# Scores of two heads in the two 64-row halves of TensorE, the projection's sums spread over steps, and two small sums moved

## The chip, the cores and the metric

The kernel runs on one core of a Trainium2 chip. A core has a matrix engine (PE, with its weight loads PEld shown apart), VectorE (DVE), ScalarE (ACT), GpSimd (POOL) and queues that start DMA transfers (SP's here, and ACT's for the output). The metric is the device time of one execution in microseconds (us); the median of several runs counts.

## The reference, cut to what matters

```
# r, k, v: (4, 8, 768, 48) float32;  w, u: (8, 48)
for t in range(S):
    cur = einsum('bhd,bhe->bhde', u * k_t, v_t)
    y[:, :, t] = einsum('bhd,bhde->bhe', r_t, state + cur)
    state = w * state + einsum('bhd,bhe->bhde', k_t, v_t)
x = y as (3072, 384)
out = (silu(x @ w_gate) * (x @ w_val)) @ w_out     # d_ff = 1536
```

The weights are between 0.85 and 0.95, so the recurrence can be done in chunks of 128 time steps with scaled copies of k and r.

## The kernel before, in words

**Chunks.** There are 24 chunks `i`: 6 stretches of 128 time steps times 4 batches, and chunk `i` works on batch `i % 4`. For a chunk, POOL makes `khat = k * kscale` and `rhat = r * rscale` (function `scale`, L274 and L275; `kscale` and `rscale` hold powers of w and are made once at the start). `turn` (L300 to L308) transposes both on PE, two heads at a time: a pair is 2 x 48 = 96 columns, so the transposed `kT` and `rT` have 96 rows, 48 of each head. ACT copies them out of PSUM. For `kT` it does so twice (L303), once per head of the pair, scaling each time by a column of `own`, which is 1 on the rows of that head and 0 on the other's.

**Scores.** `scores(i, half)` multiplies four such zeroed `kT` by `rT` (L314, 128 columns out, 96 rows deep), and DVE copies what lies on the right side of the diagonal into `At` (`copy_predicated`, L318). `diagonal` has filled `At` before with the sums `du` on the diagonal (L291 on ACT, eight heads each). `own_product` makes `rk = r * k * u` on POOL (L202, L203) and sums it over a head's 48 numbers on DVE (L205) into `du`, both at the same place of the program.

**Outputs and state.** `outputs` (L344) multiplies `At` by v and `rT` by the state `Z` in four 32-column strips of PE, which a line of code addresses by 32 rows of the result each. `update` (L357 on PE, L367 or L369 on DVE, L370 on POOL) adds the chunk's keys and values to `Z`.

**The second block.** 12 groups `g` of two chunks go through `gate_value` (L390 on PE, L396 on ACT, L397 and L398 on DVE) and `project` (L453). The projection is done with seven products of half blocks instead of eight. This needs four sums of the weight's blocks, made once (`weight_sums`, L414 to L417 on POOL, 1152 numbers a row each), and four sums of h's blocks for each group (`h_sums`, L432 to L435 on POOL, for the last group on DVE).

**The weights** come as 64-bit floats and are rounded to 32 bits in 18 parts on the core: ACT (L162, L166), DVE (L179, L180) and POOL (L190), a part at a time. `round_weights` advances this by one part. It writes to a PSUM tile `w_mag` of which there is one.

**The order** is written out by hand: every engine executes its instructions in the order in which the program calls them. Step `s` calls, in this order: `diagonal(s-1)`, `own_product(s+1)`, `scale(s+1)`, `turn(s)`, `scores(s-1)` in two halves, `outputs(s-2)` and `update(s-2)`. Between these stand `gaps`, which hold pieces of the second block (`feed`, taken from the list `todo`) and, in steps 3 to 11, rounding of weights:

```
EARLY = {s: ("R", "F", "R", "F", "RF") for s in range(3, 12)}
```

R is `round_weights`, F one piece of `todo`. From step 12 on the five gaps hold 3, 2, 2, 3 and 2 pieces. A piece of `todo` waits until enough weights are rounded; those that need the sums of the weights wait for `NW + 1`, that is for `weight_sums` to stand in the program.

`ps_a` has four PSUM buffers that the tiles `tp` (twice), `s_ps` (twice), `y_ps` and `u_ps` of a step take in turn, so `y_ps` takes the buffer that the transposed `khat` of its step had, and the next `tp` those of the scores.

Of the kernel before, what the change touches and what calls it, by code (L numbers as in the profile page):

```python
# [15 lines left out]
P = 128  # L16
# [6 lines left out]
def fast(  # L23
# [44 lines left out]
    wcol = cst.tile([D2, HP], FP32, name="wcol")  # L68
# [3 lines left out]
    own = cst.tile([D2, 2], FP32, name="own")  # L72
    wL = cst.tile([D2, HP, 2, D], FP32, name="wL")
    sq = cst.tile([D2, 8, HP], FP32, name="sq")
    bad = cst.tile([D2, HP], FP32, name="bad")
    held = cst.tile([D2, HP], FP32, name="held")
    badc = cst.tile([D2, 1], FP32, name="badc")
    ones = cst.tile([D2, 1], FP32, name="ones")
# [7 lines left out]
    Z = [cst.tile([D2, HP, D2], FP32, name=f"Z{b}") for b in range(B)]  # L86
# [110 lines left out]
    dus = {}  # L197

    def own_product(i):
        kl, rl = k_ld[i % 2], r_ld[i % 2]  # L200
        rk = two.tile([P, H, D], FP32, name="rk", tag="rk")
        pool.tensor_mul(rk[:], rl[:], kl[:])  # L202
        pool.tensor_mul(rk[:], rk[:], ub[:])  # L203
        du = three.tile([P, H], FP32, name="du", tag="du")
        dve.tensor_reduce(du[:], rk[:], axis=AX.X, op=ALU.add)  # L205
        dus[i] = du
# [3 lines left out]
    for t in v_ld:  # L210
        dve.memset(t[:, :, D:64], 0.0)
    for e in range(2):
        sp.dma_start(out=wcol[D * e : D * e + D, :], in_=w.rearrange("(a e) d -> e d a", e=2)[e])
# [23 lines left out]
    for step, base in ((-D, 0), (D, D - 1)):  # L237
# [8 lines left out]
    pw = two.tile([D2, HP, P + 1], FP32, name="pw", tag="hT")  # L246
    dve.memset(pw[:, :, P : P + 1], 1.0)
    dve.tensor_copy(pw[:, :, P - 1 : P], held[:].unsqueeze(2))
    for l in range(7):
        n = 1 << l  # L250
        f = sq[:, l, :].unsqueeze(2).to_broadcast([D2, HP, n])
        dve.tensor_mul(pw[:, :, P - 2 * n : P - n], pw[:, :, P - n : P], f)
    for n in (1, 0):
        t_ps = ps_a.tile([P, HP, D2], FP32, name="t_ps", tag="a")
        for a in range(HP):
            pe.transpose(t_ps[:, a, :], pw[:, a, n : n + P], ident[0:D2, 0:D2])
        x = t_ps[:].rearrange("p a x -> p (a x)")
        if n:
            act.copy(kscale[:].rearrange("p h d -> p (h d)"), x)
        else:  # L260
            dve.reciprocal(rscale[:].rearrange("p h d -> p (h d)"), x)
    own_product(0)
    own_product(1)

# [8 lines left out]
    def scale(i):  # L273
        pool.tensor_mul(khat[i % 4][:], k_ld[i % 2][:], kscale[:])  # L274
        pool.tensor_mul(rhat[i % 2][:], r_ld[i % 2][:], rscale[:])  # L275
# [20 lines left out]
    def turn(i):  # L296
        for nm, t in (("kT", khat[i % 4]), ("rT", rhat[i % 2])):
            tp = ps_a.tile([P, HP, P], FP32, name="tp", tag="a")
            for a in range(HP):
                pe.transpose(tp[0:D2, a, :], pair(t, a), ident[:])  # L300
            if nm == "kT":
                for e in range(2):
                    act.activation(  # L303
                        kT[i % 2][:, :, e, :], tp[0:D2], AF.Identity, scale=own[:, e : e + 1]
                    )
            else:
                turned[i] = three.tile([D2, HP, P], FP32, name=nm, tag=nm)
                act.copy(turned[i][:], tp[0:D2])  # L308

    def scores(i, half):  # L310
        ps = ps_a.tile([P, HP, P], FP32, name="s_ps", tag="a")
        for n in range(4):
            a, e = divmod(4 * half + n, 2)
            pe.matmul(  # L314
                ps[:, n, :], kT[i % 2][:, a, e, :], turned[i][:, a, :],
                start=True, stop=True, skip_group_check=True,
            )
        dve.copy_predicated(  # L318
            At[i % 2][:, 4 * half : 4 * half + 4],
            mask[:].bitcast(INT32).unsqueeze(1).to_broadcast([P, HP, P]), ps[:],  # L320
        )
# [28 lines left out]
    def update(i):  # L350
# [4 lines left out]
        ps = ps_a.tile([D2, HP, D2], FP32, name="u_ps", tag="a")  # L355
# [15 lines left out]

    def count_outside():

        dve.tensor_tensor(bad[:], held[:], wcol[:], ALU.not_equal)
        dve.tensor_reduce(badc[:], bad[:], axis=AX.X, op=ALU.add)
        dve.memset(ones[:], 1.0)
        n_ps = ps_a.tile([P, HP, P], FP32, name="n_ps", tag="a")
        pe.matmul(n_ps[0:1, 0, 0:1], badc[:], ones[:], start=True, stop=True)
        act.copy(outside, n_ps[0:1, 0, 0:1])
# [33 lines left out]
    def weight_sums():  # L413
        pool.tensor_sub(wt[1][:], w22, w12)  # L414
        pool.tensor_sub(w12, w12, w11)
        pool.tensor_sub(wt[0][:], w22, w12)
        pool.tensor_sub(wt[2][:], w21, wt[0][:])  # L417
# [8 lines left out]
    def h_sums(g, by):  # L426
        a, b = (
            three.tile([P, 2, FH, P], FP32, name=n, tag="w_bits") for n in ("hs12", "hs34")
        )
        h11, h12, h21, h22 = h_quarters(g)  # L430
        s1, s2, s3, s4 = a[:, 0], a[:, 1], b[:, 0], b[:, 1]
        by.tensor_add(s1, h22, h21)  # L432
        by.tensor_sub(s2, s1, h11)
        by.tensor_sub(s3, h11, h21)
        by.tensor_sub(s4, h12, s2)  # L435
        part_of[g] = {"s": (s1, s2, s3, s4)}
# [556 lines left out]
```

## Time and profile before

| what | value |
|---|---|
| median of 3 runs (lowest, highest) | 706.93 us (706.92, 707.24) |
| the profiled execution: its time, its span | 708.06 us, 706.3 us |
| mean granted TensorE clock | 0.988 |
| DVE, ACT, POOL busy | 240.7 us (34%), 204.4 us (29%), 237.1 us (34%) |
| scores L314: matmul records | 384, 51.3 us |
| outputs L344: matmul records | 768 with `At`, 480 with `Z` |
| state L357: matmul records | 160, 16.6 us |

One matmul of 32-bit floats stands in the trace as two records, one for each of two passes, with two weight loads; a transpose stands as one. A record's duration has the depth of the array in it and overlaps the next one's. What a group of matmuls takes out of PE's time is the distance from its first start to the start of what follows, and it is that distance which is used below. "idle before ... <- X" says what ended a wait. The span is counted from the first to the last instruction.

### The profile page before, as it was taken

The numbers are of one execution on the slowest core, as the hardware profiler recorded it, in microseconds if no ns is written. First come the engines' busy times: TensorE is split into PE (matmuls) and PEld (weight loads), VectorE is DVE, ScalarE is ACT, GpSimd is POOL, SyncE is SP. The second block draws the span as 40 slices with busy tenths as digits, with TensorE's granted clock in tenths as the row PEclk, the third lists the DMA queues.
The fourth block names the chain that finished last, engine by engine and source line by source line (L and its number), as shares of the span: only waits on it lengthen the run. The fifth ranks groups of instructions, "written<-read, shape, count | busy, mean of one in ns | idle before, by whom it ended". The sixth has DMA issues, their size and how long they took to land.

```text
span 706.3 us, 11610 instructions
## 1 busy us (share of the span) xinstructions
PE 681.0 (96%) x4822; PEld 620.2 (88%) x4822; DVE 240.7 (34%) x519; ACT 204.4 (29%) x522; POOL 237.1 (34%) x191
## 2 busy tenths in 40 slices
PE   8888997999899999999999999999999999999996
PEld 8777886898798998999999999999898998998996
DVE  5777772313222222323222322323222322222222
ACT  3577762442132231313131331313131211111110
POOL 6877678358203320602512420602400400304000
PEclk9998998999999999999999999999999999999999
DMA  8798831113001010102011110001000000000000
GB/s 236 196 240 226 204 76 34 35 35 78 17 18 46 12 34 23 34 1 57 12 23 35 23 35 23 12 1 35 1 1 23 1 1 23 1 17 7 1 23 26
DMA packets 85774, 34.07 MB, mean 48 GB/s; under 512 B 76368, under 2 KB 79568, under 8 KB 85712
## 3 DMA queue, kind: packets, MB, share of 16 engines
q1 hardware_dynamic: 82256, 28.52, 17.3%
q10 hardware_dynamic: 3456, 4.72, 1.8%
q8 instruction: 40, 0.66, 0.4%
q14 instruction: 22, 0.18, 0.1%
HBM read 28.51 MB, written 4.72 MB: 47 GB/s over the span
## 4 chain that ended last, share of the span: by engine, by line
PE 81%; DVE 6%; POOL 5%; ACT 5%; issue 1%; DMA 1%; SPq 0%; DVEq 0%; POOLq 0%
PE gv L390 47%; PE o_a L453 13%; PE o_b L453 10%; PE y_ps L344 4%; PE s_ps L314 4%; PE tp L300 2%; ACT At L291 2%; ACT w_mag L162 1%; PE u_ps L357 1%; DVE At L318 1%; ACT kT L303 1%; DVE hT L398 1%; DVE sg L397 1%; DVE wg L180 1%; DMA r_ld<-in_r_dram 1%
## 5 line engine op out<-in xcount | busy, mean ns | idle before, releaser
L390 PE MATMUL gv<-xT,wg 128*128 128x256 f32 x864 | 216.0, 387 | 4.0 <-DVE hT L398 4.0
L390 PE MATMUL gv<-xT,wv 128*128 128x256 f32 x864 | 211.6, 381 | 0.0
L390 PEld LDWEIGHTS gv<-xT,wv 128*128 128x128 f32 x864 | 165.5, 192 | 22.9
L390 PEld LDWEIGHTS gv<-xT,wg 128*128 128x128 f32 x864 | 159.7, 193 | 25.8 <-issue 7.7
L397 DVE TENSOR_TENSOR sg<-sg,gv 128x256 f32<-128x256 f32 x144 | 60.5, 420 | 348.2 <-ACT sg L396 347.8
L396 ACT ACTIVATE sg<-gv 128x256 f32<-128x256 f32 x144 | 55.0, 382 | 345.9 <-PE gv L390 345.8
L432 POOL TENSOR_TENSOR hs<-hT 128x768 f32<-128x768 f32 x11 | 19.9, 1809 | 195.6 <-DVE hT L398 195.6
L370 POOL TENSOR_TENSOR Z<-Z,wL 96x384 f32<-96x384 f32 x16 | 15.9, 995 | 191.7 <-DVE Z L369 191.7
L398 DVE TENSOR_TENSOR hT<-sg,gv 128x256 f32<-128x256 f32 x144 | 60.6, 421 | 5.1
L291 ACT ACTIVATE At<-ident,du 128x128 f32<-128x128 f32 x176 | 53.6, 389 | 0.0
L314 PE MATMUL s_ps<-rT,kT 96*128 96x128 f32 x384 | 51.3, 278 | 0.4 <-DVE Z L367 0.4
L453 PE MATMUL o_a<-wt,hs 128*128 128x192 f32 x288 | 50.9, 327 | 0.4 <-ACT u L461 0.4
L314 PEld LDWEIGHTS s_ps<-rT,kT 96*128 96x128 f32 x384 | 49.5, 194 | 1.5 <-DVE Z L367 0.7
L453 PE MATMUL o_b<-wo,hs 128*128 128x192 f32 x288 | 50.7, 326 | 0.0
L453 PEld LDWEIGHTS o_a<-wt,hs 128*128 128x128 f32 x288 | 47.5, 190 | 1.5 <-ACT u L461 0.7
L453 PEld LDWEIGHTS o_b<-wo,hs 128*128 128x128 f32 x288 | 47.6, 190 | 0.8
L318 DVE COPY_PREDICATED At<-mask,s_ps 128x512 f32<-128x512 int32 x48 | 35.0, 733 | 24.4 <-PE s_ps L314 24.4
L344 PE MATMUL y_ps<-At,v_ld 128*32 128x128 f32 x768 | 36.1, 279 | 5.8 <-ACT kT L303 4.4
L344 PEld LDWEIGHTS y_ps<-At,v_ld 128*32 128x32 f32 x768 | 29.9, 111 | 6.6 <-ACT kT L303 4.6
L344 PE MATMUL y_ps<-rT,Z 96*32 96x128 f32 x480 | 30.2, 278 | 1.7 <-ACT kT L303 1.7
L303 ACT ACTIVATE kT<-tp,own 96x512 f32<-96x512 f32 x48 | 29.8, 672 | 0.0
L162 ACT ACTIVATE w_mag<-w_bits 128x384 f32<-128x384 f32 x36 | 19.0, 529 | 24.3 <-DVE wg L180 11.0
(82 smaller groups left out, 639.2 us busy)
## 6 DMA issues: line engine op xcount, KB each, us to landing
k_ld<-in_k_dram SPq DMA_DIRECT2D x24, 192.0 KB, 2.9
r_ld<-in_r_dram SPq DMA_DIRECT2D x24, 192.0 KB, 3.3
w_bits<-in_moe_w_gate_dram SPq DMA_DIRECT2D x6, 768.0 KB, 5.1
v_ld<-in_v_dram SPq DMA_DIRECT2D x48, 96.0 KB, 2.8
w_bits<-in_moe_w_val_dram SPq DMA_DIRECT2D x6, 768.0 KB, 4.7
w_bits<-in_moe_w_out_dram SPq DMA_DIRECT2D x6, 768.0 KB, 4.5
out_dram<-o_sb ACTq DMA_DIRECT2D x24, 192.0 KB, 1.9
ub<-in_u_dram SPq DMA_DIRECT2D x1, 192.0 KB, 3.7
```

Of the source, the lines that this page charges most:

```text
L162: act.activation(mags[n][-1].bitcast(FP32), hi.bitcast(FP32), AF.Abs, scale=float(2.0**-112))
L291: act.activation(At[i % 2][:, h, :], ident[:], AF.Identity, scale=du[:, h : h + 1])
L303: act.activation(kT[i % 2][:, :, e, :], tp[0:D2], AF.Identity, scale=own[:, e : e + 1])
L314: pe.matmul(ps[:, n, :], kT[i % 2][:, a, e, :], turned[i][:, a, :], start=True, stop=True, skip_group_check=True,)
L318: dve.copy_predicated(At[i % 2][:, 4 * half : 4 * half + 4], mask[:].bitcast(INT32).unsqueeze(1).to_broadcast([P, HP, P]), ps[:],)
L344: pe.matmul(ps[32 * q : 32 * q + 32, cc, :], *rows[q][n], start=(n == 0), stop=(n == len(rows[q]) - 1), skip_group_check=True,)
L390: pe.matmul(gv[:, o, :].rearrange("p (i t) -> p i t", i=2), wt[:, c, P * f : P * (f + 1)], xT[:, 2 * g % NX : 2 * g % NX + 2, c, :], start ...
L396: act.activation(sg[:], gv[:, 0, :], AF.Sigmoid)
L397: dve.tensor_mul(sg[:], sg[:], gv[:, 0, :])
L398: dve.tensor_mul(hT[g][:, f, :], sg[:], gv[:, 1, :])
L432: by.tensor_add(s1, h22, h21)
L453: pe.matmul(ps[:], lhs[:, f, :], rhs[:, f, :], start=(f == 0 and n in (0, 1, 4)), stop=(f == FH - 1), skip_group_check=True,)
```

## The change

Six things are changed together.

1. Heads lie in 64 rows instead of 48. `khat` and `rhat` get 64 columns a head, the last 16 zero (six `memset` on DVE at the start); the transposed pair has 128 rows, head 0 on rows 0 to 47 and head 1 on rows 64 to 111. `kT` is copied out once, without `own`. `scores(i)` does both halves of the chunk in one go: eight products that are 48 rows deep, in turn on rows 0 to 47 and 64 to 111, and each row half writes to its own PSUM tile. `wcol`, `own`, `wL`, `sq`, `held`, `pw` and `Z` are 128 rows high (`wcol` is filled with ones on DVE before its DMA).
2. In `update` the stationary operand, the pair of `khat`, has 128 columns instead of 96.
3. The sum `du` leaves `own_product`: `own_sum(s)` stands at the end of step `s`, before the last gap, one step after the product on POOL and before `diagonal(s)` in step `s + 1`.
4. The four sums of weights are four pieces, taken at R places once all parts are rounded, and what needs them waits for all four (`NW + 4`). R and F now stand in steps 3 to 12.
5. `h_sums` is two pieces of `todo`, with two sums each.
6. The count of w outside its limits: its DVE part stands at the start, and only its matmul and copy stay in step 12.

```diff
@@ tiles
-    khat = [cst.tile([P, H, D], FP32, name=f"khat{i}") for i in range(4)]
-    rhat = [cst.tile([P, H, D], FP32, name=f"rhat{i}") for i in range(2)]
+    khat = [cst.tile([P, H, 64], FP32, name=f"khat{i}") for i in range(4)]
+    rhat = [cst.tile([P, H, 64], FP32, name=f"rhat{i}") for i in range(2)]
-    kT = [cst.tile([D2, HP, 2, P], FP32, name=f"kT{i}") for i in range(2)]
+    kT = [cst.tile([P, HP, P], FP32, name=f"kT{i}") for i in range(2)]
...
@@ start
+    def own_sum(i):
+        dus[i] = three.tile([P, H], FP32, name="du", tag="du")
+        dve.tensor_reduce(dus[i][:], rks.pop(i)[:], axis=AX.X, op=ALU.add)
...
+    for t in khat + rhat:
+        dve.memset(t[:, :, D:64], 0.0)
+    dve.memset(wcol[:], 1.0)
     for e in range(2):
-        sp.dma_start(out=wcol[D * e : D * e + D, :], in_=w.rearrange("(a e) d -> e d a", e=2)[e])
+        sp.dma_start(out=wcol[64 * e : 64 * e + D, :], in_=w.rearrange("(a e) d -> e d a", e=2)[e])
...
@@ turn and scores
-                pe.transpose(tp[0:D2, a, :], pair(t, a), ident[:])
+                pe.transpose(tp[:, a, :], pair(t, a), ident[:])
             if nm == "kT":
-                for e in range(2):
-                    act.activation(
-                        kT[i % 2][:, :, e, :], tp[0:D2], AF.Identity, scale=own[:, e : e + 1]
-                    )
+                act.copy(kT[i % 2][:], tp[:])
...
+    def scores(i):
+        ps = [ps_a.tile([P, HP, P], FP32, name="s_ps", tag="a") for _ in range(2)]
+        for a in range(HP):
+            for e in range(2):
+                rows = slice(64 * e, 64 * e + D)
+                pe.matmul(
+                    ps[e][:, a, :], kT[i % 2][rows, a, :], turned[i][rows, a, :],
+                    start=True, stop=True, skip_group_check=True,
+                )
+        for e in range(2):
+            dve.copy_predicated(
+                At[i % 2][:].rearrange("p (a e) t -> p a e t", e=2)[:, :, e],
+                mask[:].bitcast(INT32).unsqueeze(1).to_broadcast([P, HP, P]), ps[e][:],
             )
...
@@ sums
-    def weight_sums():
+    def weight_sum():
+        n = len(summed)
+        o = (wt[1][:], w12, wt[0][:], wt[2][:])[n]
+        a, b = ((w22, w12), (w12, w11), (w22, w12), (w21, wt[0][:]))[n]
+        pool.tensor_sub(o, a, b)
+        summed.append(n)
...
             if what == "R":
-                round_weights()
+                if done["pool"] < NW:
+                    round_weights()
+                elif len(summed) < 4:
+                    weight_sum()
...
-    EARLY = {s: ("R", "F", "R", "F", "RF") for s in range(3, 12)}
+    EARLY = {s: ("R", "F", "R", "F", "RF") for s in range(3, 13)}
+    dve.tensor_tensor(bad[:], held[:], wcol[:], ALU.not_equal)
+    dve.tensor_reduce(badc[:], bad[:], axis=AX.X, op=ALU.add)
+    dve.memset(ones[:], 1.0)
...
@@ the loop over steps
         if s <= N:
-            scores(s - 1, 0)
+            scores(s - 1)
             gaps(s, 1)
-            scores(s - 1, 1)
...
             update(s - 2)
+        if s < N:
+            own_sum(s)
         gaps(s, 4)
```

Three places show how the rows move. On PE, this is step 7 before, from its transposes (`tp` from `khat` and `rhat`) over the scores (`s_ps`) to the state (`u_ps`); `gv` is a piece of the second block:

```order
L300 MATMUL tp<-ident,khat_114 96x128 x4
L300 MATMUL tp<-ident,rhat_116 96x128 x4
L314 MATMUL s_ps<-rT,kT_119 128x128 x4
L390 MATMUL gv<-xT,wg 128x256 x3
L390 MATMUL gv<-xT,wv 128x256 x3
L314 MATMUL s_ps<-rT,kT_119 128x128 x4
L344 MATMUL y_ps<-rT,Z_100 32x128 x4
```

The same place of the changed program:

```order
L308 MATMUL tp<-ident,khat_114 128x128 x4
L308 MATMUL tp<-ident,rhat_116 128x128 x4
L321 MATMUL s_ps<-rT,kT_119 128x128 x8
L389 MATMUL gv<-xT,wg 128x256 x3
L389 MATMUL gv<-xT,wv 128x256 x3
L352 MATMUL y_ps<-rT,Z_100 32x128 x4
```

The eight products of a chunk stand together, and between them and the outputs, which use 32-column strips, stands a piece of full height and width.

On POOL, this is the end of step 7 and step 8 before, with the sums of weights (`wt`, and `wo` in place) behind the last rounding and the state's product `Z`:

```order
L190 TENSOR_TENSOR wo<-wo,w_low 128x768 x2
L370 TENSOR_TENSOR Z_100<-Z_100,wL 96x384
L414 TENSOR_TENSOR wt_214<-wo 128x1152
L415 TENSOR_TENSOR wo<-wo 128x6x192
L416 TENSOR_TENSOR wt_213<-wo 128x1152
L417 TENSOR_TENSOR wt_215<-wo,wt_213 128x1152
L202 TENSOR_TENSOR rk<-r_ld_104,k_ld_106 128x384
L203 TENSOR_TENSOR rk<-rk,ub 128x384
L274 TENSOR_TENSOR khat_112<-k_ld_106,kscale 128x384
L275 TENSOR_TENSOR rhat_116<-r_ld_104,rscale 128x384
L370 TENSOR_TENSOR Z_101<-Z_101,wL 96x384
```

And in the changed program:

```order
L191 TENSOR_TENSOR wo<-wo,w_low 128x768 x2
L378 TENSOR_TENSOR Z_100<-Z_100,wL 128x384
L417 TENSOR_TENSOR wt_221<-wo 128x1152
L203 TENSOR_TENSOR rk<-r_ld_104,k_ld_106 128x384
L204 TENSOR_TENSOR rk<-rk,ub 128x384
L282 TENSOR_TENSOR khat_112<-k_ld_106,kscale 128x8x48
L283 TENSOR_TENSOR rhat_116<-r_ld_104,rscale 128x8x48
L417 TENSOR_TENSOR wo<-wo 128x6x192
L417 TENSOR_TENSOR wt_220<-wo 128x1152
L378 TENSOR_TENSOR Z_101<-Z_101,wL 128x384
L417 TENSOR_TENSOR wt_222<-wo,wt_220 128x1152
```

One sum stays ahead of the next chunk's products `rk`, `khat` and `rhat`, and three stand behind them.

On DVE, this is the start of step 8 before: the state's sum of step 7, a piece of the second block (`sg`, `hT`), the sum `du` of the chunk whose `rk` POOL makes in this same step, and the copies of the scores:

```order
L369 TENSOR_TENSOR Z_100<-u_ps,Z_100 96x384
L397 TENSOR_TENSOR sg<-sg,gv 128x256
L398 TENSOR_TENSOR hT<-sg,gv 128x256
L205 TENSOR_REDUCE du<-rk 128x8
L318 COPY_PREDICATED At_118<-mask,s_ps 128x512
```

In the changed program:

```order
L377 TENSOR_TENSOR Z_100<-u_ps,Z_100 128x384
L209 TENSOR_REDUCE du<-rk 128x8
L396 TENSOR_TENSOR sg<-sg,gv 128x256
L397 TENSOR_TENSOR hT<-sg,gv 128x256
L326 COPY_PREDICATED At_118<-mask,s_ps 128x4x128 x2
```

The sum stands two rows earlier, and it is that of the chunk whose `rk` was made one step before.

More of the change, by code (lines that the diff above doesn't have):

```diff
@@ L273, in scale @@
     def scale(i):
-        pool.tensor_mul(khat[i % 4][:], k_ld[i % 2][:], kscale[:])
-        pool.tensor_mul(rhat[i % 2][:], r_ld[i % 2][:], rscale[:])
+        pool.tensor_mul(khat[i % 4][:, :, 0:D], k_ld[i % 2][:], kscale[:])
+        pool.tensor_mul(rhat[i % 2][:, :, 0:D], r_ld[i % 2][:], rscale[:])
         if i >= 2:
@@ L547, in fast @@
     update(1)
+    own_sum(2)
     round_weights()
@@ L568, in fast @@
             update(s - 2)
+        if s < N:
+            own_sum(s)
         gaps(s, 4)
         if s == 12:
-            count_outside()
-        if done["pool"] == NW and not summed:
-            summed.append(True)
-            weight_sums()
+            n_ps = ps_a.tile([P, HP, P], FP32, name="n_ps", tag="a")
+            pe.matmul(n_ps[0:1, 0, 0:1], badc[:], ones[:], start=True, stop=True)
+            act.copy(outside, n_ps[0:1, 0, 0:1])
     assert done["pool"] == NW
     feed(len(todo))
-    h_sums(N // 2 - 1, dve)
+    h_sums(N // 2 - 1, 0, dve)
+    h_sums(N // 2 - 1, 1, dve)
     for p in range(7):
```

117 lines of the change are left out of this document (49 added, 68 removed).

## The prediction, made before the changed kernel ran

> **What bounds the kernel.** I read the page first: busy shares, granted clock by slices, and the chain of waits by engine.
>
> ```profile
> span 706.3 us, 11610 instructions
> PE 681.0 (96%) x4822; PEld 620.2 (88%) x4822; DVE 240.7 (34%) x519; ACT 204.4 (29%) x522; POOL 237.1 (34%) x191
> PEclk9998998999999999999999999999999999999999
> PE 81%; DVE 6%; POOL 5%; ACT 5%; issue 1%; DMA 1%; SPq 0%; DVEq 0%; POOLq 0%
> ```
>
> PE is busy in 96% of the span; the clock falls in a few early slices only. A table of three stretches (start:end, length, busy time of each engine, clock) tells where the other 4% are.
>
> ```profile
> 50.00:62.00 12.00, 7.57 (x59) 6.10 (x58) 9.44 (x19) 9.65 (x23) 9.20 (x7) 0.72 0.94 246
> 114.00:126.00 12.00, 8.00 (x33) 6.50 (x32) 4.09 (x9) 1.17 (x4) 9.85 (x10) 0.72 0.25 49
> 200.00:680.00 480.00, 480.00 (x3211) 438.78 (x3211) 130.01 (x295) 101.86 (x280) 108.07 (x81) 1.00 0.07 18
> ```
>
> From 200 to 680 us PE never pauses and no other engine is busy for over 28% of the time: what PE saves there comes off the end one for one, and what it gains in work is paid. At 50 to 62 us four engines share the limit, at 114 to 126 us POOL has the most work, and in both the clock is 0.72. PE's waits, one row per cause:
>
> ```profile
> PE y_ps L344 <- ACT kT L303: 6.1, 3, 4.4
> PE gv L390 <- DVE hT L398: 4.0, 1, 4.0
> PE n_ps L378 <- DVE ones L376: 1.8, 1, 1.8
> PE tp L300 <- DVE At L318: 1.7, 1, 1.7
> ```
>
> So there are two things to win: PE's own work, and these waits (us in total, times, longest).
>
> **The scores on PE.** PE's order of time in steps 4 and 5, after the waits of step 4 (start, duration, records):
>
> ```profile
> 61.57 0.84 PE L357 MATMUL u_ps<-v_ld,khat 128*96 128x96 f32 x8
> 62.25 1.49 PE L390 MATMUL gv<-xT,wg 128*128 128x256 f32 x6
> ...
> 64.87 0.60 PE L300 MATMUL tp<-ident,khat 128*96 128x128 f32 x4
> 65.30 0.60 PE L300 MATMUL tp<-ident,rhat 128*96 128x128 f32 x4
> 65.74 1.06 PE L314 MATMUL s_ps<-rT,kT 96*128 96x128 f32 x8
> 66.63 1.46 PE L390 MATMUL gv<-xT,wg 128*128 128x256 f32 x6
> ...
> 69.23 1.06 PE L314 MATMUL s_ps<-rT,kT 96*128 96x128 f32 x8
> 70.21 1.10 PE L344 MATMUL y_ps<-At,v_ld 128*32 128x128 f32 x32
> 71.25 1.56 PE L390 MATMUL gv<-xT,wg 128*128 128x256 f32 x6
> 72.65 1.46 PE L390 MATMUL gv<-xT,wv 128*128 128x256 f32 x6
> ```
>
> Half the scores take 66.63 - 65.74 = 0.89 us, 0.111 for each of 8 records, so a step pays 1.78 us. The new form has the same 16 records on half the rows. No row shows two row halves at work; the nearest are the outputs, whose 32 records in four 32-column strips take 71.25 - 70.21 = 1.04 us. Eight in a row in one strip would take 8 x 0.111 = 0.89, so four strips do run side by side, weight loads too:
>
> ```profile
> 110.48 0.16 PEld L344 LDWEIGHTS y_ps<-rT,Z 96*32 96x32 f32 x8
> L314 PEld LDWEIGHTS s_ps<-rT,kT 96*128 96x128 f32 x384 | 49.5, 194 | 1.5 <-DVE Z L367 0.7
> L344 PEld LDWEIGHTS y_ps<-At,v_ld 128*32 128x32 f32 x768 | 29.9, 111 | 6.6 <-ACT kT L303 4.6
> ```
>
> Eight loads of 0.1 us each lie within 0.16 us. I take row halves to behave alike: a body of 8 x 0.111 = 0.89 us. Going into strips and out again isn't free. The scores ahead of the outputs last 70.21 - 69.23 = 0.98 instead of 0.89 (+0.09); the outputs 1.04 instead of 0.89 (+0.15); the first half of the piece behind them 72.65 - 71.25 = 1.40 instead of 1.30, half of 69.23 - 66.63 (+0.10). That is 0.34 a visit, with a first load of 32 columns in the open; one of 128 columns is 194 - 111 = 83 ns longer, so 0.42. A block costs 0.89 + 0.42 = **1.31 us instead of 1.78**, 0.47 less; in the 20 steps 5 to 24 that is **-9.4 us**. From both sides: without a price for the visit 0.89 (-17.8 in all); with all 16 loads in a row 2.20 (+8.4).
>
> The Trainium skill speaks against the change here: "TensorEngine Tiling (Array Packing)", Key Properties, says that changing the tiling mode drains TensorE. The trace agrees: 0.34 us a visit in the rows above. Without that rule the term would be -17.8, with it -9.4.
>
> **State.** The weights of `u_ps` grow from 96 to 128 columns. Eight records with 96 columns on both sides take 62.25 - 61.57 = 0.68 us, 0.085 each; scores, 128 on both sides, take 0.111. Which side sets that isn't shown. Load durations grow with columns (111 ns for 32, 194 for 128), so I take 0.111: +0.21 us in 17 updates (steps 5 to 21), **+3.6**. If the 96 moving columns set it, 0. Transposes keep 128 moving columns; 0.
>
> **The stall in step 8.** `du` on DVE waits for `rk`, which stands on POOL behind four sums of weights, and behind `du` wait the products that free PE's buffers.
>
> ```profile
> 104.83 2.62 POOL L414 TENSOR_TENSOR wt<-wo 128x1152 f32<-128x1152 f32 x1
> ...
> 115.54 0.99 POOL L202 TENSOR_TENSOR rk<-r_ld,k_ld 128x384 f32<-128x384 f32 x1
> 117.63 0.55 DVE L205 TENSOR_REDUCE du<-rk 128x8 f32<-128x384 f32 x1 [11.00 <-POOL rk L203]
> 114.87 0.84 PE L357 MATMUL u_ps<-v_ld,khat 128*96 128x96 f32 x8
> 119.72 2.90 PE L390 MATMUL gv<-xT,wg 128*128 128x256 f32 x6 [4.00 <-DVE hT L398]
> ...
> 124.97 0.85 PE L300 MATMUL tp<-ident,khat 128*96 128x128 f32 x4
> ```
>
> Without it the transposes would start at 114.87 + 0.68 + 2.60 = 118.15, not 124.97: 6.8 us, of which 4.0 is the wait and the rest the half clock after it; the transposes themselves are slow too. I take **-7.0**. In the new order one sum stands ahead of `rk` and DVE asks for `rk` a step later. POOL's work in step 8 is 4 x 1.0 for the next chunk, 3 x 2.63, and 1.0 for `Z`: 12.9 us, near the step's 13. What is due next step (`khat`, `rhat`) stands ahead of the three sums, so nothing is late. On DVE `du` now stands behind the state's sum, and `diagonal` and the copies of the transposes wait for it on ACT; at 130 busy us in 480 DVE has the room, and I count 0.
>
> **Two more waits.** In step 12 the transposes wait for `At`, again behind a `du` that POOL's h sums hold up.
>
> ```profile
> 157.81 2.14 PE L453 MATMUL o_a<-wt,hs 128*128 128x192 f32 x12
> 160.30 0.55 DVE L205 TENSOR_REDUCE du<-rk 128x8 f32<-128x384 f32 x1 [10.35 <-POOL rk L203]
> 161.64 0.61 PE L300 MATMUL tp<-ident,khat 128*96 128x128 f32 x4 [1.69 <-DVE At L318]
> ```
>
> **-2.0** with the slow transposes after it. The `n_ps` wait of 1.8 (row above) goes, since its DVE part is done at the start: **-1.9**. New is that steps 10 to 12 have little on PE: transposes 0.87, scores 1.31, outputs about 1.9, state 0.89 and two projections of 1.96 (12 records at 157.81), 8.9 us. POOL has 4.0 + 1.0 + 3.6 with half of the h sums, 8.6. A late `khat` could cost 0 to 2 us; **+0.3**.
>
> **The start.** Six more `memset` and the ones in `wcol` come before the first DMA, and behind that stand SP's loads of k, r, u and weights.
>
> ```profile
> 0.80 0.89 SPq L213 DMA_DIRECT2D wcol<-in_w_dram  x2
> 0.88 0.33 DVE L211 MEMSET v_ld<- 128x64 f32 x4 [0.88 <-PEq L977]
> 26.77 0.55 DVE L205 TENSOR_REDUCE du<-rk 128x8 f32<-128x384 f32 x1 [2.71 <-POOL rk L203]
> L303 ACT ACTIVATE kT<-tp,own 96x512 f32<-96x512 f32 x48 | 29.8, 672 | 0.0
> L308 ACT COPY rT<-tp 96x512 f32<-96x512 f32 x24 | 13.8, 573 | 0.0
> ```
>
> Four of 64 numbers take 0.33 us; six of 128 at twice that each would take 1.0, so the DMA starts near 2.2 instead of 0.8: +1.3, and 0.5 for the DVE rows of the count. Against it, DVE's 2.71 us wait for `rk` goes, and ACT copies `kT` once, 0.57 instead of 1.34 us a step. That is the engine for which PE waits 4.4 us in step 4, and 1.7 in two later steps together. PE saves work there too, which it will only wait out. Ends: +1.8, if nothing is made up, to -7, if the 4.4 and most of the half clock behind them go. The delays and savings listed nearly cancel by step 3; I take **-1.0**.
>
> **Sum:** -9.4 + 3.6 - 7.0 - 2.0 - 1.9 + 0.3 - 1.0 = -17.4. The profiled execution took 708.06 us, 1.13 over the median of the runs, 706.93; from the median the forecast is 706.93 - 17.4 = **689.5 us**.
>
> **Rivals.** (1) *The halves take turns.* If their weight loads share one way in, a block is 16 x 0.111 + 0.42 = 2.20 us, and the sum is -17.4 + 20 x 0.89 = +0.4: 707.3. If each product also waits for its load, 32 x 0.111 + 0.42 = 3.97, +53 more than forecast: 743. This is also the case in which "side by side" isn't true. It turns the sign from 1.31 + 17.4 / 20 = 2.18 us a block on. Against it are the strips above; for it, that strips load few columns each and halves load all 128. The Trainium skill, "TensorE: Matmul & The Clock Gate", LDWEIGHTS, says that a load's time goes by columns and not by rows, so a half's load would not be shorter. The trace agrees as to columns (111 and 194 ns); it doesn't show two row halves. (2) *The stalls come back.* POOL's 12.9 us in step 8, or a late `khat`, hold PE as before: without the -7.0 and -2.0 it is 698.5. Against it: PE is the only engine with no slack from 200 us on, and `du` has a step's room. (3) *The state's loads are hidden,* 0 instead of +3.6: 685.9.
>
> **Chances.** Forecast 0.58, halves in turn 0.11 (its lighter form 0.08), stalls back 0.14, state free 0.17. The forecast's own range is 685 to 694 by the ends of the start; with (3) and a better start 682, with (2) and some of the start's price 702. Rival (1) is left out. About 0.2% (1.4 us) is what a measurement of this kernel can tell from no change: faster 0.89, same 0.03, slower 0.08, nearly all of the last two from (1).
>
> **What would show it.** A step's scores from first start to the next piece at 1.2 to 1.4 us: right; 2.2: rival 1. `u_ps` at 0.89 for 8 records, or 0.68. No wait of PE over 1 us after 62 us, and a clock of 1.0 at 114 to 126; if POOL's `rk` or `khat` releases PE there, rival 2. PE's first wait for `pw` about 1.3 us longer. I am wrong in kind if PE pauses in the stretch in which it was full, or if the clock falls there.

## The result, and the profile after

The changed kernel takes **691.56 us** (median of 4 runs, 691.40 to 691.94); the kernel before took 706.95 us beside it. The ratio is 0.9782, with a 95% interval of 0.9765 to 0.9799. The forecast was 689.5 us, with a range of 682 to 702.

| what | before | after |
|---|---|---|
| the profiled execution: its time, its span | 708.06 us, 706.3 us | 691.46 us, 689.6 us |
| mean granted TensorE clock | 0.988 | 0.994 |
| scores: matmul records | 384, 51.3 us | 384, 28.3 us |
| state: matmul records | 160, 16.6 us | 160, 20.5 us |

The page of the changed kernel: span, busy time and share of each engine, granted clock in 40 slices, and the chain that ended last.

```profile
span 689.6 us, 11591 instructions
PE 668.0 (97%) x4822; PEld 600.2 (87%) x4822; DVE 235.5 (34%) x526; ACT 188.7 (27%) x498; POOL 238.0 (35%) x191
PEclk9999999999999999999999999999999999999999
PE 86%; DVE 6%; ACT 5%; issue 1%; POOL 1%; DMA 1%; SPq 0%; DVEq 0%; ACTq 0%; POOLq 0%
```

PE is still the engine that sets the end: it has 13 us less work and the chain lies on it for 86% instead of 81%. The first two stretches of the prediction again (columns as there):

```profile
50.00:62.00 12.00, 6.54 (x54) 5.12 (x52) 8.90 (x18) 8.54 (x21) 9.11 (x7) 0.86 0.94 241
114.00:126.00 12.00, 12.00 (x122) 10.35 (x121) 4.82 (x10) 4.91 (x14) 9.80 (x7) 1.00 0.25 48
```

From 114 to 126 us, where the stall of step 8 lay, PE is busy all the time at full clock. From 50 to 62 us PE gets no further than before: it has 54 records there instead of 59, and is busy for 6.54 us instead of 7.57 at a clock of 0.86 instead of 0.72. The longest of PE's waits (us in total, times, longest) has grown.

```profile
PE y_ps L352 <- ACT kT L310: 7.6, 3, 5.5
```

The waits before of 4.0 us for `hT`, 1.8 before `n_ps` and 1.7 for `At` are gone. The wait for ACT's `kT` in step 4 has grown from 4.4 to 5.5 us; of this more below. Ahead of it, at 24.96 us, `y_ps` waits 2.8 us for `At`, where the longest such wait before was 1.3: the first `w_mag` of the rounding starts at 12.64 us instead of 10.88. By step 4 that is made up, for its transposes start at 44.22 instead of 45.49. PE's order of time in steps 4 and 5 (start, duration, records):

```profile
61.44 1.03 PE L365 MATMUL u_ps<-v_ld,khat 128*128 128x96 f32 x8
62.31 1.49 PE L389 MATMUL gv<-xT,wg 128*128 128x256 f32 x6
...
64.92 0.60 PE L308 MATMUL tp<-ident,khat 128*128 128x128 f32 x4
65.36 0.60 PE L308 MATMUL tp<-ident,rhat 128*128 128x128 f32 x4
65.89 1.16 PE L321 MATMUL s_ps<-rT,kT 48*128 48x128 f32 x16
66.98 1.56 PE L389 MATMUL gv<-xT,wg 128*128 128x256 f32 x6
68.38 1.46 PE L389 MATMUL gv<-xT,wv 128*128 128x256 f32 x6
```

The 16 records of the scores take 66.98 - 65.89 = 1.09 us. The way in costs 0.09 (65.89 - 65.36 = 0.53; 0.44 before) and the first half of the piece behind 0.10 (68.38 - 66.98 = 1.40; 1.30 elsewhere). That is **1.28 us a step instead of 1.78**, 0.50 less; forecast was 0.47. `u_ps` takes 62.31 - 61.44 = 0.87 instead of 0.68, 0.19 more; forecast was 0.21.

To see where the 16.7 us between the two spans lie, one mark is enough: the start of the transposes of steps 8 and 9. Before:

```profile
105.14 0.60 PE L300 MATMUL tp<-ident,khat 128*96 128x128 f32 x4
...
124.97 0.85 PE L300 MATMUL tp<-ident,khat 128*96 128x128 f32 x4
```

After:

```profile
104.95 0.60 PE L308 MATMUL tp<-ident,khat 128*128 128x128 f32 x4
...
117.67 0.60 PE L308 MATMUL tp<-ident,khat 128*128 128x128 f32 x4
```

| stretch | before | after | difference |
|---|---|---|---|
| to step 8 | 105.14 | 104.95 | -0.2 |
| step 8 | 19.83 | 12.72 | -7.1 |
| step 9 to the end of the span | 581.3 | 571.9 | -9.4 |

In steps 9 to 24 the scores give 16 x 0.50 = 8.0 and the state takes 13 x 0.19 = 2.5; with the two small waits (3.5 to 3.9) that makes the last row. Step 8 is the stall, and its own scores and state (-0.3). What is missing is the first row: three cheaper blocks of scores, less three dearer ones of state, and the start were to give 3 x 0.47 - 3 x 0.21 + 1.0 = 1.8 us there, and gave 0.2. Step 5 begins at 64.92 instead of 64.87, so the start gave nothing; and of the 0.9 us that scores and state should save in steps 5 to 7 at the prices just measured, 0.2 are seen.

### The profile page after: what moved, and what is told of

It is laid out like the page before. It is cut to its first block, busy times and chain, and to the rows that moved or that the text cites. A ratio compares the mean times of both kernels' runs of the same rounds, so it can differ in the third digit from the quotient of the medians.

```text
span 689.6 us, 11591 instructions
## 1 busy us (share of the span) xinstructions
PE 668.0 (97%) x4822; PEld 600.2 (87%) x4822; DVE 235.5 (34%) x526; ACT 188.7 (27%) x498; POOL 238.0 (35%) x191
## 3 DMA queue, kind: packets, MB, share of 16 engines
q10 hardware_dynamic: 3456, 4.72, 1.8%
HBM read 28.51 MB, written 4.72 MB: 48 GB/s over the span
## 4 chain that ended last, share of the span: by engine, by line
PE 86%; DVE 6%; ACT 5%; issue 1%; POOL 1%; DMA 1%; SPq 0%; DVEq 0%; ACTq 0%; POOLq 0%
PE gv L389 50%; PE o_a L457 14%; PE o_b L457 10%; PE y_ps L352 5%; PE s_ps L321 3%; PE tp L308 2%; ACT At L299 2%; PE u_ps L365 2%; DVE At L326 1%; ACT w_mag L163 1%; DMA r_ld<-in_r_dram 1%; DVE wv L180 1%; DVE hT L397 1%; DVE wv L181 1%; DVE sg L396 1%
## 5 line engine op out<-in xcount | busy, mean ns | idle before, releaser
L378 POOL TENSOR_TENSOR Z<-Z,wL 128x384 f32<-128x384 f32 x16 | 16.0, 998 | 166.1 <-DVE Z L377 166.1
L457 PE MATMUL o_a<-wt,hs 128*128 128x192 f32 x288 | 51.3, 328 | 0.4 <-ACT u L465 0.4
L326 DVE COPY_PREDICATED At<-mask,s_ps 128x512 f32<-128x512 int32 x48 | 32.4, 729 | 15.3 <-PE s_ps L321 9.5
L352 PE MATMUL y_ps<-rT,Z 128*32 128x128 f32 x480 | 30.1, 279 | 2.3 <-ACT kT L310 2.1
L321 PEld LDWEIGHTS s_ps<-rT,kT 48*128 48x128 f32 x384 | 23.7, 187 | 6.7 <-issue 4.0
L321 PE MATMUL s_ps<-rT,kT 48*128 48x128 f32 x384 | 28.3, 284 | 1.0 <-DVE At L326 0.9
L352 PEld LDWEIGHTS y_ps<-rT,Z 128*32 128x32 f32 x480 | 19.3, 109 | 8.6 <-issue 5.2
L203 POOL TENSOR_TENSOR rk<-r_ld,k_ld 128x384 f32<-128x384 f32 x24 | 24.3, 1014 | 5.7 <-DMA r_ld<-in_r_dram 5.5
```

The costliest lines, as they stand in the source:

```text
L321: pe.matmul(ps[e][:, a, :], kT[i % 2][rows, a, :], turned[i][rows, a, :], start=True, stop=True, skip_group_check=True,)
L326: dve.copy_predicated(At[i % 2][:].rearrange("p (a e) t -> p a e t", e=2)[:, :, e], mask[:].bitcast(INT32).unsqueeze(1).to_broadcast([P, H ...
L352: pe.matmul(ps[32 * q : 32 * q + 32, cc, :], *rows[q][n], start=(n == 0), stop=(n == len(rows[q]) - 1), skip_group_check=True,)
L378: pool.tensor_mul(z[:], z[:], wL[:].rearrange("p a e d -> p a (e d)"))
L457: pe.matmul(ps[:], lhs[:, f, :], rhs[:, f, :], start=(f == 0 and n in (0, 1, 4)), stop=(f == FH - 1), skip_group_check=True,)
```

## The experiments

Twelve kernels were run, each beside the kernel before on its own chip, where that took 707.4 to 708.6 us. So ratios are compared, and "us" is the ratio times 706.95. The changed kernel stands at 0.9782 (691.56).

| kernel | ratio, 95% interval | us | expected by the theory |
|---|---|---|---|
| before, layout of the pairs alone | 0.9946, 0.9930 to 0.9963 | 703.1 | 702.5 |
| before, sums spread alone | 0.9884, 0.9868 to 0.9901 | 698.7 | 700 |
| before, count of w alone | 0.9964, 0.9950 to 0.9978 | 704.4 | 705.0 |
| before, `own_sum` alone | 1.0013, 1.0000 to 1.0026 | 707.9 | 699 |
| the same, two-input rounding | 1.0070, 1.0056 to 1.0084 | 711.9 | 702 |
| the same, at the head of the step | 0.9921, 0.9907 to 0.9935 | 701.4 | 701 |
| after, scores on all rows | 0.9937, 0.9920 to 0.9954 | 702.5 | 701.6 |
| after, halves one after another | 0.9902, 0.9886 to 0.9919 | 700.0 | 691.6 |
| after, scores next to outputs | 0.9785, 0.9768 to 0.9801 | 691.8 | 687.8 |
| after, the same from step 9 on | 0.9747, 0.9731 to 0.9763 | 689.1 | 688.5 |
| after, `wcol` first | 0.9765, 0.9745 to 0.9785 | 690.3 | 690.4 |
| after, two-input rounding | 0.9836, 0.9821 to 0.9850 | 695.4 | 690.5 |

### Are the halves side by side?

**The scores on all 128 rows**, as before the change, in the changed kernel. `kT` is copied twice again, with zeros.

```diff
-                act.copy(kT[i % 2][:], tp[:])
+                for e in range(2):
+                    act.activation(kT[i % 2][:, :, e, :], tp[:], AF.Identity, scale=own[:, e : e + 1])
...
-                    ps[e][:, a, :], kT[i % 2][rows, a, :], turned[i][rows, a, :],
+                    ps[e][:, a, :], kT[i % 2][:, a, e, :], turned[i][:, a, :],
```

> The changed kernel (691.56 us) with only the scores as before: kT copied twice with the other head's rows set to zero, eight products on all rows, in one go. Theory (the halves run side by side and are worth 1.79 - 1.29 = 0.50 us a step): 20 x 0.50 = 10 us slower, 701.6 (700.5 to 704.5, the upper end if the second copy on ACT makes the early steps longer), the scores at 1.79 us a step in the trace, u_ps still at 0.89. Rival (the gain is that of the removed stalls alone, the halves give nothing net): 691 to 693.

It takes 702.5, 11 us more than the changed kernel. PE's order of time in step 9:

```profile
123.21 1.95 PE L323 MATMUL s_ps<-rT,kT 128*128 128x128 f32 x16
125.00 1.46 PE L391 MATMUL gv<-xT,wg 128*128 128x256 f32 x6
```

A block is 1.79 us again. The span is 701.9: from step 8's transposes (at 109.12) to the end it has 592.8 us against 584.7 of the changed kernel: +8.1, near the 17 x 0.50 = 8.5 of steps 8 to 24. The other 4.2 us lie ahead of step 8, where three blocks of scores account for 1.5 at most. Where the rest comes from stays open: PE waits for `kT` no longer than in the changed kernel (6.6 us in all, 7.6 there), and the rest is no more than what those steps differ by anyway (below).

**The halves one after another**: the two loops in `scores` swapped, so that four products on the upper rows are followed by four on the lower.

```diff
-        for a in range(HP):
-            for e in range(2):
+        for e in range(2):
+            for a in range(HP):
```

> The changed kernel with the two loops of scores swapped: the four products of the upper half stand in a row, then the four of the lower half, instead of in turn. If each half of the rows has work of its own in hand that TensorE may run ahead, nothing changes: 691.6 (690.8 to 692.4). The rival: TensorE takes the instructions strictly in order and overlaps only neighbours, so that the halves run after one another, the block goes from 1.31 to about 2.2 us, and 20 steps add 18: 709 (705 to 711).

It takes 700.0: neither. PE in step 9:

```profile
121.98 1.71 PE L321 MATMUL s_ps<-rT,kT 48*128 48x128 f32 x16
123.62 1.56 PE L389 MATMUL gv<-xT,wg 128*128 128x256 f32 x6
```

The block is 123.62 - 121.98 = 1.64 us instead of 1.09. The starts of the single records in the trace show the reason. In each of the 20 blocks from step 5 on, the first record of the lower half starts sixth, ahead of the last three of the upper half, so not in the order of the program. Three times a record of either half start together, within 0.006 us; the other ten records start alone. In the changed kernel all 16 start in such pairs, eight of them, in 19 of the 20 blocks. Thirteen starts instead of eight, five more of 0.111, are the 0.55. It is so too in the nine blocks in which the lower half's first load waits for no semaphore, so it isn't its PSUM tile that holds it up. What sets the three records isn't shown. 20 steps at 0.55 make 11.0; the ratio gives 8.4, the spans 701.2 - 689.6 = 11.6. The rates are those of the forecast only because the program writes the halves in turn.

**The scores directly ahead of the outputs**, without a piece of full size between halves and strips.

```diff
         if s <= N:
-            scores(s - 1)
             gaps(s, 1)
         gaps(s, 2)
+        if s <= N:
+            scores(s - 1)
         if s >= 4:
             outputs(s - 2)
```

> The changed kernel with scores(s-1) directly ahead of outputs(s-2), without gate-value pieces between them. The theory: what the block costs beside its products is paid where TensorE goes from the full array to parts and back, so that going from the halves to outputs' strips directly saves one way back per step, about half of the 0.42 us that the prediction counts as overhead: 20 steps at -0.19 give 687.8 (686.5 to 689.5), if nothing else moves. The rival: a change between any two arrangements costs the same, or the overhead is the first weight load in the open, which stays: 691.6 (690.5 to 693, more where outputs wait for the masked copy of the scores, which is then late by as much as it takes).

It takes 691.8, no change; but the trace shows both a gain and a loss. The transposes of steps 8, 9 and 10 start at 109.57, 122.09 and 134.61. Step 9 is 12.52 us, 0.19 less than in the changed kernel, as the theory says; but step 8 begins 4.6 us later. So the same order from step 9 on alone:

```diff
+            if s < 9:
                 scores(s - 1)
...
+        if 9 <= s <= N:
+            scores(s - 1)
```

> The changed kernel with scores directly ahead of outputs from step 9 on, and where the change put them before. The theory from a3_next_to_outputs: the direct way from halves to strips saves 0.19 us per step (step 9 took 12.52 instead of 12.71 us there), and what a3_next_to_outputs gave back lay in steps 5 to 8, where the rounding is; so 16 steps at -0.19 give 688.5 (688.0 to 689.3). The rival: what a3_next_to_outputs gave back comes of the order itself, anywhere: 691 to 692.

It takes **689.1** by the ratio, the fastest of all; its interval ends at 0.9763, and that of the changed kernel begins at 0.9765. From step 8's transposes to the end the profiled execution has 690.4 - 108.53 = 581.9 us against 584.7: -2.8, with 3.0 expected. So about half of what a block costs beside its products (0.39) is saved where no piece of full size stands between halves and strips. Yet the execution reached step 8 at 108.53, and the changed kernel at 104.95, with the same program up to there. The five runs of this kernel go from 688.64 to 692.15. So the steps up to 8 differ by 3 us and more from one execution to another with the same instructions, and differences of 1 us in them can't be told from single traces.

### One part of the change at a time

**The layout of the pairs alone** (64-row halves, one copy of `kT`, state with 128 columns) in the kernel before.

> The kernel before, with the change's layout of the pairs alone (64-row halves, scores without kT's zeros, state products of 128 columns); the seven-product sums, the count and own_sum stay where they were. The theory: what TensorE saves per step counts only from step 9 on, since steps 2 to 8 are set by the rounding of the weights (ScalarE, VectorE and GpSimd in turn) and the stall in step 8 by GpSimd, so that TensorE gets to the same places early and waits there. 16 steps at -0.50 and 13 updates at +0.19 give -5.5; step 12's and n_ps's waits on GpSimd take about half of what comes ahead of them: 702.5 (701 to 704.5) where the kernel before takes 706.95. The rival, that the prediction's terms simply add (-9.4 + 3.6 - 1.0): 700 or less. The rival that the stalls swallow everything: 706 to 707.

It takes 703.1, as the theory says; the profiled execution (702.15 us) is the fastest of the four, the others took 704.1 to 705.0. PE in step 8:

```profile
119.86 2.90 PE L395 MATMUL gv<-xT,wg 128*128 128x256 f32 x6 [4.72 <-DVE hT L403]
```

The stall is still there, PE waits 4.72 instead of 4.0 us for it, and step 9 begins at 124.90 as before (124.97). From there to the end the span of 700.3 has 575.4 us, the kernel before 581.3: -5.9, near 16 x 0.50 - 13 x 0.19. The waits of step 12 took no part of it, unlike what was expected: they are 1.6 and 1.7 us, as before (1.7 and 1.8). What TensorE saves ahead of a stall of POOL is waited out at the stall.

**The sums alone**: the four sums of weights as four pieces, those of h as two, R and F also in step 12; code as in the change. **The count of w alone**: its three DVE instructions at the start.

> The kernel before (706.95 us) with only the weight sums as four pieces, the h sums as two, and R and F in step 12 too. Theory (one sum ahead of rk makes DVE wait about 3 us at du in step 8, not 11, and the h sums half as long in step 12): 6 + 1 us faster, 700 (698 to 702). Rival (as long as du stands where it stood, DVE holds PE): 705 or more.

> The kernel before (706.95 us) with only the DVE part of the count at the start. Theory (PE's wait of 1.8 us in step 12 ends with it, and the 0.4 us of DVE at the start is hidden or costs that): 705.0 (704.6 to 705.6). Rival (another wait takes its place): 706.9.

They take 698.7 and 704.4. With the sums spread, step 8 takes 13.3 us instead of 19.8 (its transposes start at 106.22, those of step 9 at 119.54), though `du` stands where it stood. From step 9's transposes to the end the sums alone leave 579.1 us and the count alone 579.3, where the kernel before has 581.3: 2.3 and 2.0 less, for the two small waits.

**`own_sum` alone** in the kernel before: the sum `du` of chunk `s` at the end of step `s`, directly behind the addition to `Z`.

```diff
             update(s - 2)
+        if s < N:
+            own_sum(s)
         gaps(s, 4)
```

> The kernel before (706.95 us) with only the sum du moved to the end of the step. Theory (the stall in step 8 and the wait in step 12 come from DVE standing at du): 7.1 + 2.0 less about 1.4 for khat that is made behind the four sums: 699 (697.5 to 700.5), no wait of PE for hT. Rival (POOL's four sums in a row hold PE through khat whatever DVE does): 704 or more, with a wait of PE for khat of over 4 us.

It takes 707.9: nothing is gained. That is the rival's time, but not its reason, for PE's longest wait for `khat` is 1.8 us (over 4 was said). The wait in step 12 stays as well: the transposes there wait 1.33 us for `khat` instead of 1.69 for `At`. The stall in step 8 is gone, and step 7 has one instead: its transposes start at 92.93, those of step 8 at 112.30, 19.4 us later (13.6 in the kernel before, 14.0 in the changed one). DVE, POOL and ACT in step 7:

```profile
93.00 0.55 DVE L373 TENSOR_TENSOR Z<-u_ps,Z 96x384 f32<-96x384 f32 x1
93.47 0.54 DVE L208 TENSOR_REDUCE du<-rk 128x8 f32<-128x384 f32 x1
93.93 2.74 DVE L179 TENSOR_SCALAR wo<-w_bits 128x384 int32<-128x384 int32 x1
...
93.62 1.05 POOL L374 TENSOR_TENSOR Z<-Z,wL 96x384 f32<-96x384 f32 x1 [3.75 <-DVE Z L373]
94.64 1.81 POOL L190 TENSOR_TENSOR wo<-wo,w_low 128x768 int32<-128x768 int32 x1
...
97.36 0.53 ACT L162 ACTIVATE w_mag<-w_bits 128x384 f32<-128x384 f32 x1 [3.88 <-DVE wo L180]
98.08 2.43 ACT L295 ACTIVATE At<-ident,du 128x128 f32<-128x128 f32 x8
100.42 1.24 ACT L307 ACTIVATE kT<-tp,own 96x512 f32<-96x512 f32 x2
...
101.72 0.65 PE L348 MATMUL y_ps<-rT,Z 96*32 96x128 f32 x8 [3.37 <-ACT kT L307]
104.86 2.93 PE L394 MATMUL gv<-xT,wg 128*128 128x256 f32 x6
```

Read from the top: DVE's addition to `Z` releases POOL's product, which starts at 93.62. Without `du` the rounding's L179 would start at 93.47, ahead of POOL, and last 0.35 us; that this is so shows in the run with `du` at the head of the step, below. With `du` it starts at 93.93, beside POOL, and ends at 96.67, when POOL's two instructions are over. ACT's next `w_mag`, which needs its turn, is 3.88 us late, and in order behind it stand `At` and `kT`; PE waits 3.37 us, and its next piece runs at half the pace (2.93 us for six records, elsewhere 1.5).

Two ways to test this. **First the instruction's form**: the rounding's sign taken by an instruction with two tensor inputs, in this kernel and in the changed one.

```diff
-        dve.tensor_scalar(dst, hi, -(1 << 31), None, ALU.bitwise_and)
+        dve.scalar_tensor_tensor(dst, hi, -(1 << 31), hi, ALU.bitwise_and, ALU.bitwise_and)
```

> The kernel before, with own_sum moved (as in b1_own_sum) and, in the rounding of the weights, the sign taken by an instruction with two tensor inputs (hi & mask & hi) instead of tensor_scalar; the values are the same. The theory: in b1_own_sum the stall of step 8 was gone, and the time was given back because a tensor_scalar of the rounding lasted 2.74 us beside a running GpSimd instruction (0.35 alone), while the two-input form lasts 0.56 us whatever GpSimd does; so step 7 goes back from 19.4 to about 14 us, step 8 stays without its stall, and the time is 702 (700 to 704.5) where the kernel before takes 706.95. The rival: moving du costs VectorE or the rounding itself what it gains, whatever form the rounding has: 707 or more.

> The changed kernel with the two-input form in the rounding. The theory: 36 instructions of 0.56 us (20.2 us) instead of 21.5 us with some of 1.8 to 2.0 us; the long ones hold up the chain to step 8, the short ones lie in slack: 690.5 (689.3 to 691.8). The rival: the chain is bound by every instruction of the rounding, 27 of the 36 get 0.15 us longer, and the kernel slower by 2 to 4 us: 693.5 to 695.5.

Both missed: 711.9 and 695.4, slower by 4 us each, where the rivals had put them. The theory of the form falls, since this form is held up in the same way. The same instruction in step 7 of the first of the two, which takes 20.0 us there:

```profile
96.39 3.14 DVE L179 SCALAR_TENSOR_TENSOR wo<-w_bits 128x384 int32<-128x384 int32 x1
```

From the changed kernel, the two instructions of its rounding by the tile that they write (ns min/median/max):

```profile
L180 DVE TENSOR_SCALAR wv<-w_bits x12: 415/420/1976, 20.5 to 71.1; 128x384 int32<-128x384 int32 x12
L181 DVE SCALAR_TENSOR_TENSOR wv<-w_mag,wv x12: 557/558/560, 22.6 to 71.8; 128x384 int32<-128x384 int32 x12
```

and from the changed kernel with the two-input form:

```profile
L180 DVE SCALAR_TENSOR_TENSOR wv<-w_bits x12: 546/730/2112, 21.5 to 74.3; 128x384 int32<-128x384 int32 x12
```

L181 never changes, the other does in both forms. L181 has `w_mag`, in PSUM, as an input; the two-input form has both in SBUF. The Trainium skill, "SBUF — State Buffer", "SBUF: two separate sides", says that VectorE instructions with two inputs in SBUF, or in a mode that uses two ports, and GpSimd's take turns on a pair of ports, each for a whole instruction. The trace agrees for L181 (557 to 560 ns) and for the two-input form (up to 2112). In the traces the long ones end with POOL: the seven of L180 over 0.65 us in the changed kernel end 0.21 to 0.29 us behind the end of an instruction of POOL, and all 24 in the kernel with the two-input form 0.41 to 0.42 us behind one. What the two runs show besides is another thing. In the changed kernel with the two-input form step 8 begins at 109.31 instead of 104.95 and the rest takes as long as ever (584.8 us): with longer instructions in the rounding, 4.4 us more up to step 8. The ratio says the same in all runs together, 3.8 us more. The rounding sets the pace there.

**Then the place**: the same `du`, at the head of the step, where the kernel before sums that of the next chunk.

```diff
             scale(s + 1)
+        if s < N:
+            own_sum(s)
         if s < N:
             turn(s)
...
-        if s < N:
-            own_sum(s)
         gaps(s, 4)
```

> b1_own_sum with own_sum(s) at the head of its step, where the kernel before had the sum of du, instead of directly behind update's addition to Z. The theory, after b5_own_sum_two_input took the form of the instruction out as a cause: it is the place. Behind the addition to Z, du (0.54 us) puts the rounding's next VectorE instruction behind the start of GpSimd's product with Z, which that addition releases; the instruction then lasts until GpSimd's work is done (2.74 us in step 7), ScalarE's next w_mag waits 3.88 us for it, kT is 3 us late and TensorE waits and goes to half clock. At the head of the step the instruction ahead of w_mag starts before GpSimd again, step 7 takes 13.6 us as in the kernel before, and step 8 keeps what the move of du gains: 701 (699 to 703) where the kernel before takes 706.95. The rival: the stall of step 8 turns up somewhere ahead of it wherever du stands, since it is the rounding that decides: 706 or more.

It takes 701.4, 6.5 us less than with `du` at the end of the step. The same place in step 7:

```profile
91.55 0.35 DVE L179 TENSOR_SCALAR wo<-w_bits 128x384 int32<-128x384 int32 x1
92.00 0.56 DVE L180 SCALAR_TENSOR_TENSOR wo<-w_mag,wo 128x384 int32<-128x384 int32 x1
92.48 2.28 DVE L179 TENSOR_SCALAR wo<-w_bits 128x384 int32<-128x384 int32 x1
...
91.71 1.04 POOL L374 TENSOR_TENSOR Z<-Z,wL 96x384 f32<-96x384 f32 x1 [3.74 <-DVE Z L373]
...
92.59 0.53 ACT L162 ACTIVATE w_mag<-w_bits 128x384 f32<-128x384 f32 x1 [1.02 <-DVE wo L180]
```

The first L179 starts ahead of POOL and lasts 0.35 us, ACT's `w_mag` follows at once, and only the next L179 is held up, without making the step longer. Step 7 takes 13.6 us and step 8 13.5.

With this in hand the changed kernel's step 4 reads otherwise. DVE, ACT and PE there:

```profile
49.52 0.54 DVE L209 TENSOR_REDUCE du<-rk 128x8 f32<-128x384 f32 x1
49.98 1.82 DVE L180 TENSOR_SCALAR wv<-w_bits 128x384 int32<-128x384 int32 x1
...
52.49 0.52 ACT L163 ACTIVATE w_mag<-w_bits 128x384 f32<-128x384 f32 x1 [1.49 <-DVE wv L181]
...
55.55 0.56 ACT L310 COPY kT<-tp 128x512 f32<-128x512 f32 x1
...
56.16 1.94 PE L352 MATMUL y_ps<-At,v_ld 128*32 128x128 f32 x32 [5.46 <-ACT kT L310]
```

And the same of ACT before:

```profile
51.01 0.49 ACT L162 ACTIVATE w_mag<-w_bits 128x384 f32<-128x384 f32 x1
...
54.05 1.24 ACT L303 ACTIVATE kT<-tp,own 96x512 f32<-96x512 f32 x2
```

Up to `du` the two traces are level: the L181 ahead of it starts at 49.04, the same row before at 49.15. Then `du` stands ahead of a held L180 here too, `w_mag` comes 1.48 us later than before, and `kT` is copied at 55.55 instead of 54.05. What the shorter copy saves (0.7) is less than that, and so the wait grew. The changed kernel with `du` at the head of the step was not tried, nor with `du` where the kernel before has it, so what the move of `du` is worth beside the spread sums isn't shown.

### The start

**`wcol` first**: its `memset` ahead of the others, so that the first transfer starts at 0.96 instead of 2.10 us.

```diff
+    dve.memset(wcol[:], 1.0)
     for t in v_ld:
...
-    dve.memset(wcol[:], 1.0)
```

> The changed kernel with the memset of wcol ahead of the memsets of v_ld, khat and rhat, so that the first transfer, which the change moved from 0.80 to 2.10 us, starts at about 1 us again. The theory: the steps to step 8 are set by the chain of rounding the weights, which begins with these transfers, so that the whole program moves by what the transfers gain: -1.1, 690.4 (689.8 to 691.0). The rival: there is slack between the transfers and the first thing that TensorE waits for: 691.6 (691.2 to 692.0).

It takes 690.3, but the interval, 0.9745 to 0.9785, holds both answers: inconclusive. The first transfers of weights ate most of what was won; ACT's first `w_mag` started at 12.29 us where the changed kernel has 12.64.

## Why the prediction was right, and where it was not

- **Scores, -9.4: right in kind and nearly in size.** Halves do run side by side, as the strips did: 1.28 us a step measured, 1.31 forecast, 20 x 0.50 = -10.0, of which the 16 steps from 9 on show in full in the time. The 0.42 us for a visit were 0.39 (1.28 less a body of 0.89). Rival (1), the halves in turn, is excluded in the form in which the program writes them; with the loops swapped 0.55 of its 0.89 us a block come true.
- **State, +3.6: right.** 17 x 0.19 = +3.2; 128 columns of weights set the pace, and rival (3) falls.
- **The stall in step 8, -7.0: right in size**, -6.8 without the step's own scores and state. The prediction gave it two causes, and either cure is enough: with the sums spread alone the step takes 13.3 us, with `du` asked for later alone 13.5.
- **"DVE has the room, and I count 0" for the new place of `du`: wrong as a step.** The room was read from 200 to 680 us, where there is no rounding. In the kernel before, that place costs 6.5 us (707.9 against 701.4). In the changed kernel its trace shows 1.5 us for it, in step 4.
- **The two small waits, -3.9 with +0.3 for a late `khat`: right.** After 62 us PE waits 2.1 us for `kT` (1.7 before), 0.4 for `u` and 0.2 for `At`, and never for `khat`. By themselves the sums were worth 2.3 us from step 9 on and the count 2.0. For step 12 the h sums are the cure and not the later `du`: with that alone PE waits there for `khat`.
- **The start, -1.0: its reason was wrong, and nothing came of it (0.0 in the two profiled executions, at step 5).** The term took the shorter copy of `kT` to relieve the wait of 4.4 us in step 4; the wait became 5.5, since `kT` comes late there by its place behind the rounding's `w_mag`, which stands 1.5 us later behind `du` and the held L180. The shorter copy gives 0.7 of that back. That without the new place of `du` the term would have come out is argued, not run. What the later first transfer adds stays open: the run that took it back was inconclusive.
- **Steps 5 to 7: counted in full, and nearly all waited out.** The sum takes 20 steps of scores and 17 of state one for one, but that PE never pauses was read from 200 us on. Steps 5 to 7 took 40.03 us instead of 40.27 (104.95 - 64.92 and 105.14 - 64.87): 0.2 of 0.9, with PE's waits for `kT` there at 2.1 us instead of 1.7. Both this and the start are differences of 1 us in steps that differ by 3 us between executions, so their sizes hold for these two traces alone.
- **The signs.** Blocks of 1.28 us and `u_ps` at 0.87 came as said, and so did a clock of 1.0 from 114 to 126 us. PE's first wait for `pw` is 1.0 us longer (1.7 instead of 0.7), where 1.3 was said. "No wait over 1 us after 62 us" was not met: one of 1.2 us for `kT` is left, as before. From 200 to 680 us PE is busy for 479.6 us; the pause of 0.4 is the wait for `u`, which lay behind 680 us before.
- **The median.** The terms were summed against an execution of 708.06 us and taken from a median of 706.93. Of the 2.0 us between forecast and result, 1.1 are this and 0.7 are the terms: by the spans, 706.3 - 17.4 = 688.9 against 689.6.

## What to carry to other kernels

Products that use part of TensorE's rows can run side by side, weight loads too, but in full only if the program writes the parts in turn; and each visit has a price, of which one piece is saved by placing two kinds of partial products next to each other. What TensorE saves ahead of a stall of another engine is waited out there, so count a saving only in the steps that TensorE bounds. An instruction of half a microsecond that is put between one engine's release of another and its own next work can cost ten times its length: read the room of an engine in the stretch in question, and look at what starts beside it.

## What the runs showed of the hardware that was not expected

- VectorE's `tensor_scalar` on 384 numbers lasts 0.35 us, or up to 2.74 beside GpSimd's work, until just after an instruction of GpSimd ends, and the profile counts all of it as busy time; with one input in PSUM an instruction of the same size lasts 0.56 us in all 36 cases.
- Row halves written one after another still overlap in part: a block takes 1.64 us, between 1.09 written in turn and 1.79 on all rows. Three of a half's eight records lie beside one of the other half.
- The same instructions reached step 8 at 104.95 us in one execution and at 108.53 in another.
